# A decay vector fetched as one row and spread by three matmuls, in an attention and MLP kernel

## The chip, the core and the metric

The kernel runs on one core of one Trainium2 chip. The metric is the device time of one execution in microseconds (us). The core has five engines that run side by side, each with its own instruction queue: TensorE (PE, matmuls; its weight loads are listed as PEld), VectorE (DVE), ScalarE (ACT), GpSimd (POOL) and SyncE (SP, which here only issues transfers). Transfers run on 16 DMA engines. "SPq" and "ACTq" are the queues on which SP and ACT issue transfers.

## The reference

Two stages. First, linear attention with decay: 4 batches, 8 heads, 768 positions, 64 columns a head. Each head h has a decay `lam[h]` between 0.97 and 0.99. In blocks of 64 positions,

```
Dmask = where(rel >= 0, lam ** rel, 0)                 # rel = i - j inside a block
intra = ((q_b @ k_b.T) * Dmask) @ v_b
inter = (q_b * lam ** (pos + 1)) @ kv_state
out_b = intra + inter
kv_state = lam ** 64 * kv_state + (k_b * lam ** (63 - pos)).T @ v_b
```

The result, 3072 tokens of 512 columns, then goes through a two-layer MLP: `h = x @ w_in` (512 to 2048), `g = 0` below -1, `h` above 1, `(h + 1)^2 / 4` between, and `out = g @ w_out` (2048 to 512). Everything is float32 outside; the kernel computes in bfloat16 with float32 sums.

## The kernel before

The decay is folded into q and k: q is multiplied by `lam ** pos` and k by `lam ** -pos`, with pos counted from the middle of the 768 positions; the mask inside a chunk is then only causal. The powers come from tables. `lam` is loaded to all 128 partitions (`lam_b`, lines 92 and 93, a broadcast read issued by ACT), ACT takes its logarithm (`ln_lam`, L104), and `tables` (lines 111 to 118) makes two pairs of tables: DVE multiplies the logarithm by positions (`arg`, L113), ACT takes the exponentials (`tk`, L115, for k, and `tq`, L117, for q). The pair with suffix "e" serves the first stage below, the pair with suffix "d" all later chunks.

The work goes in this order:

- Units 0 to 3 (functions with the prefix `e_`) cover the first 512 positions of batch 0, in two halves of positions and two halves of heads. Each unit loads q, k and v on SP's queue (`e_load`, L302, tiles x0f, x1f, x2f, 256 KB each), casts them to bfloat16 with the tables (`e_cast`, L313 and L315: k on DVE, q and mostly v on POOL), transposes q and k on PE (`e_t`, L329), copies them back (L336), then computes scores (L373), masks them on DVE (L381), updates the state (L349), and sums the output (L393, L408) into `xT` (L419).
- Chunks 4 to 23 (prefix `f_`) cover the rest in 128 positions each, with loads at L426.
- The MLP runs in six strips of 512 tokens: first layer `f_l1` (L606) with its activation on ACT (L614) and DVE (L622 to L630), second layer `f_l2` (L639), results on L664 and stores. The weights are loaded by POOL (`load_w`, L152 for w_in, L153 for w_out, nine slices); the first slice waits for the landing of unit 2's k.

The order is not left to a scheduler: every step is entered with `add(...)` with its engine, an assumed duration, what it needs and a due time. `run_plan` (lines 174 to 267) plays this forward and issues the instructions in the order that comes out. The constants that concern the change: `DMA0` (L160), the planned time in ns at which the loads' stream begins; `T0` (L678), the due time of the first MLP step, from which nearly all due times are counted; the dictionary passed to `run_plan` (L884), when each engine is first free; and `WARM` (L269). Before and between PE's first planned steps, `run_plan` issues matmuls on zeros (`warm`, L275, "warm-ups"), from `WARM[0]` on, 512 columns each where there is room and 128 otherwise, until 200 ns before the next planned step on PE.

PSUM is divided into pools; `pp_h` (two banks) holds the warm-ups' output and later the first layer's, `pp_o` (one bank) the transposes of k and some attention outputs.

Of the kernel before, what the change touches and what calls it, by code (L numbers as in the profile page):

```python
# [8 lines left out]
F32 = mybir.dt.float32  # L9
BF16 = mybir.dt.bfloat16  # L10
I32 = mybir.dt.int32
AX = mybir.AluOpType
AF = mybir.ActivationFunctionType
# [10 lines left out]
def kernel(  # L24
# [16 lines left out]
    nc = tc.nc  # L41
    B, H, S, D = q.shape
# [8 lines left out]
    MS = 512  # L51
# [7 lines left out]
    RW, NR = 2, 3  # L59
    XT, MG, NQT, NQK, NVS, NUB, RING = 6, 6, 4, 4, 5, 4, 3.5  # L60
    DBG = False
    OB = 8

    const = ctx.enter_context(tc.tile_pool(name="const", bufs=1))
# [10 lines left out]
    rp = ctx.enter_context(tc.tile_pool(name="rp", bufs=NR))  # L75
    op = ctx.enter_context(tc.tile_pool(name="op", bufs=OB))
    PS = bass.MemoryType.PSUM
    pp_h = ctx.enter_context(tc.tile_pool(name="pp_h", bufs=2, space=PS))
# [3 lines left out]
    pp_o = ctx.enter_context(tc.tile_pool(name="pp_o", bufs=1, space=PS))  # L82
# [6 lines left out]
    SYNC = mybir.DependencyInfo(mybir.DependencyClass.Sync, mybir.DependencyReason.DATA)  # L89

    nc.scalar.preload_act_table_set("natural_log_exp_and_others")
    lam_b = const.tile([128, H], F32)
    nc.scalar.dma_start(out=lam_b, in_=lam.partition_broadcast(128))


    NE = 4
# [3 lines left out]
    make_identity(nc, ident)  # L100
    zz = const.tile([128, MS], BF16)
    nc.vector.memset(zz, 0.0)
    ln_lam = const.tile([128, H], F32)
    nc.scalar.activation(out=ln_lam, in_=lam_b, func=AF.Ln)  # L104
    pos_e = const.tile([128, NE], F32)
    nc.vector.tensor_copy(pos_e, pos_ei.rearrange("p a b -> p (a b)"))
    one = const.tile([128, 1], F32)
    nc.vector.memset(one, 1.0)  # L108


    def tables(pos, n, name):
# [11 lines left out]
    for t, base in ((mask2, 0), (mask2b, 128)):  # L123
        nc.gpsimd.memset(t, 1.0)
        nc.gpsimd.affine_select(
            out=t, in_=t, compare_op=AX.is_ge, fill=0.0,
# [7 lines left out]
        out=causal, in_=causal, compare_op=AX.is_ge, fill=0.0,  # L134
# [22 lines left out]


    LAT, FILL, SWITCH, NEAR = 100, 170, 105, 4000
    LEAD_Q, TAIL_Q, DMA0 = {"SP": 1300, "POOL": 1900}, 800, 3850  # L160
    ops, OPS = [], {}

    class Op:
# [5 lines left out]
    def add(key, eng, ns, fn, needs=(), due=None, extra=0, dma=0, perf=False, mode=("full", "full"), ring=1, slack=0, late=0):  # L169
        OPS[key] = Op(key, eng, ns, fn, list(needs), due, extra, dma, perf, mode, ring, slack)  # L170
        OPS[key].late = late
        ops.append(OPS[key])

    def run_plan(free):
# [42 lines left out]
        while len(out_seq) < len(ops):  # L217
# [33 lines left out]
            for u in users[x.key]:  # L251
                left[u.key] -= 1
                if left[u.key] == 0:
                    ready[u.eng].append(u)
        at, n1 = WARM[0], 0
        for t, _, x in sorted(out_seq, key=lambda p: p[:2]):
            if x.eng == "PE" and n1 < 2:
                while at < t - (200 if at < WARM[1] else WARM[2]):
                    one_ns = 58 if at > WARM[1] else 110
                    n = 4 if at + 4 * one_ns < t - 200 else 1  # L260
                    warm(n)
                    at += n * one_ns
                at = t + x.ns
                n1 += x.key[0] == "l1"
            if DBG:
                print(f"{t / 1e3:9.3f} {min(x.due, 9e6) / 1e3:9.3f} {x.eng:5s} {x.ns:6.0f} {x.end / 1e3:9.3f} {x.key}")
            x.fn()

    WARM = (1400, 7500, 700)  # L269
    wbank = []  # L270

    def warm(n):
        if not wbank:
            wbank.append(pp_h.tile([128, MS], F32, name="ph", tag="ph"))
        nc.tensor.matmul(wbank[0][:, 0:128 * n], lhsT=zz[:, 0:128], rhs=zz[:, 0:128 * n], start=True, stop=True, skip_group_check=True)  # L275

    def mm(*cols):
        return sum(c / 2.4 + 3 for c in cols)

# [372 lines left out]
    def f_ylast(part):  # L652
        cs = slice(CUT, d_model) if part else slice(0, CUT)
        if part == 0:
            osb["last"] = op.tile([128, d_model], F32, name="osb", tag="osb")
        nc.scalar.copy(out=osb["last"][:, cs], in_=py_t["last", part][:, cs])

    def f_stlast(part):
        cs = slice(CUT, d_model) if part else slice(0, CUT)
        nc.sync.dma_start(out=out[n_tok - 128:n_tok, cs], in_=osb["last"][:, cs])  # L660

    def f_y(s, ms):
        osb[s, ms] = op.tile([128, d_model], F32, name="osb", tag="osb")
        nc.scalar.copy(out=osb[s, ms], in_=py_t[s, ms])  # L664

    def f_out(s, ms):
        m0 = s * MS + ms * 128
        if s == 0:

            for j in range(2):  # L670
                nc.gpsimd.dma_start(out=out[m0:m0 + 128, :].rearrange("(p j) n -> j p n", j=2)[j], in_=osb[s, ms][HD[j], :])
        elif s < NST - 1:
            nc.gpsimd.dma_start(out=out[m0:m0 + 128, :], in_=osb[s, ms])  # L673
        else:
            nc.sync.dma_start(out=out[m0:m0 + 128, :], in_=osb[s, ms])


    T0, STEP, LEAD = 17000, 1035, 3000  # L678
    PARTS = {0: 2, 1: 4, 2: 2, 3: 2, 4: 2, 5: 2}
    W0 = [(w, p) for w in range(4) for p in range(2)]  # L680
    ALONE, AHEAD, AHEAD2 = 16, 6, 11
# [154 lines left out]
    for n1, (_, s, i, p) in enumerate(l1_order):  # L836
        prev = bank[on_y[n1]]
        n = PARTS.get(s, 1)
# [18 lines left out]
    for n2, (_, s, ms, kg) in enumerate(l2_order):  # L857
        n = PARTS.get(s, 1)
# [5 lines left out]
        if y == NCH - 1:  # L864
            if kg == 0:
                for part, n in ((0, CUT), (1, d_model - CUT)):
# [3 lines left out]
                    add(("y", y + part), "ACT", 400 - 240 * part, lambda part=part: f_ylast(part),  # L870
                        [("last", part), ("y", y - 1 + part), ("st", y - OB)], extra=95)
                    add(("st", y + part), "SP", 550 if s else 1100, lambda part=part: f_stlast(part), [("y", y + part), ("st", y - 1 + part)], due=-1,
# [5 lines left out]
        if kg == 3:  # L878
            add(("y", y), "ACT", 490, lambda a=(s, ms): f_y(*a), [("l2", n2), ("y", y - 1), ("st", y - OB)], extra=95)
            add(("st", y), "POOL" if s < NST - 1 else "SP", 1600 if s == 0 else 800 if s < NST - 1 else 550, lambda a=(s, ms): f_out(*a),  # L880
                [("y", y), ("o", 9 + y)] if s == 0 else [("y", y), ("st", y - 1) if y > CPS else None],
                due=l_due[2, s, ms, kg] + OLATE if s < NST - 1 else -1, dma=650, ring=0.2, slack=OSLACK if s < NST - 1 else 0)

    run_plan({"PE": 5000, "ACT": 5000, "DVE": 5000, "POOL": 5000, "SP": 800})  # L884


# [28 lines left out]
```

## Time and profile before

| what | value |
|---|---|
| time, median of 3 runs | 209.01 us (208.78 to 209.41) |
| time of the profiled execution | 210.35 us |
| its span, first to last instruction | 208.6 us |
| PE busy | 201.6 us, 97% of the span |
| DVE, ACT, POOL busy | 140.0, 120.4, 72.8 us |
| granted PE clock, mean over the span | 0.99 |
| DMA moved | 34.49 MB, mean 165 GB/s |

How to read what follows. The page divides the span into 40 slices of 5.2 us; each digit is a busy share in tenths, and the row PEclk is the granted share of PE's full clock. The chain of waits goes back from the last instruction, at each step to what released it. A timeline line gives the start, the duration, the engine, the line of the kernel, the operation with its output and inputs, and in brackets how long the engine had been idle and what ended that. A windows line gives the window, its length, the busy time of PE, PEld, DVE, ACT and POOL with the count of instructions, the granted clock, the DMA engines' busy share and GB/s. The clock's column covers what the trace recorded; before the first record, at 6.59 us, it shows 1.00 for want of one, while the warm-ups there take 0.427 us for 512 columns.

### The profile page before, as it was taken

Reading aid. Unit: us, or ns where it says so; the run is one execution under the profiler, and the core shown is the slowest. Engines: PE = TensorE matmul, PEld = TensorE weight load, DVE = VectorE, ACT = ScalarE, POOL = GpSimd, SP = SyncE. Lnnn points to the kernel's source line nnn. Section 1 sums busy time; section 2 is a strip of 40 time slices with the busy share of each in tenths; the row PEclk is TensorE's granted clock in tenths of the full one; section 3 lists DMA queues with packets and bytes.
Section 4 is the critical chain, followed back from the end, with each engine's and each line's share of the span. In section 5 each row is a group of like instructions: output and inputs, shape, how many; then the busy total and the mean of one; then the engine's idle time right before and its main releaser. Section 6 shows DMA issues by size and latency. Waiting matters only on the chain.

```text
span 208.6 us, 6389 instructions
## 1 busy us (share of the span) xinstructions
PE 201.6 (97%) x2754; PEld 137.1 (66%) x2754; DVE 140.0 (67%) x245; ACT 120.4 (58%) x225; POOL 72.8 (35%) x95
## 2 busy tenths in 40 slices
PE   7779999999999999999999999999999999999994
PEld 2457887446866876666766767667667666666643
DVE  0575697453898786998877989976866656354510
ACT  2564675225865767585675786575675565464421
POOL 5598200145255173763554354335511011010000
PEclk9996999999999999999999999999999999999999
DMA  4999999999999999999999999999822002011112
GB/s 106 296 246 177 201 202 199 234 214 179 173 232 211 196 235 222 212 246 228 173 199 280 170 257 219 205 177 213 147 50 104 3 5 98 0 50 53 50 50 101
DMA packets 95051, 34.49 MB, mean 165 GB/s; under 512 B 82352, under 2 KB 93360, under 8 KB 95024
## 3 DMA queue, kind: packets, MB, share of 16 engines
q1 hardware_dynamic: 88464, 24.65, 65.4%
q0 software_dynamic: 6416, 9.44, 21.2%
q8 instruction: 21, 0.34, 0.7%
q14 instruction: 6, 0.05, 0.1%
q10 hardware_dynamic: 144, 0.00, 0.0%
HBM read 27.27 MB, written 6.29 MB: 161 GB/s over the span
## 4 chain that ended last, share of the span: by engine, by line
PE 90%; SPq 4%; DMA 3%; ACT 1%; issue 1%; DVE 0%; ACTq 0%
PE ph L606 40%; PE py L639 39%; SPq L302 4%; DMA x1f<-in_k_dram 3%; PE py L649 2%; PE ps L500 1%; PE py L606 1%; PE ps L492 1%; PE pu L527 1%; PE po L527 1%; PE po L511 1%; PE py L408 1%; DVE ks L315 0%; PE pu L511 0%; PE py L393 0%
## 5 line engine op out<-in xcount | busy, mean ns | idle before, releaser
L606 PE MATMUL ph<-xT,w_in_sb 128*128 128x256 bf16 (+1 forms) x872 | 94.8, 258 | 0.0
L639 PE MATMUL py<-w_out_sb,gT 128*128 128x512 bf16 x368 | 91.1, 379 | 0.0
L614 ACT ACTIVATE r<-ph,one 128x512 bf16<-128x512 f32 x93 | 63.9, 687 | 46.5 <-PE ph L606 40.9
L606 PEld LDWEIGHTS <-w_in_sb 128*128 128x128 bf16 x896 | 76.7, 98 | 19.9 <-issue 0.2
L639 PEld LDWEIGHTS <-gT 128*128 128x128 bf16 x368 | 34.9, 98 | 28.4
L622 DVE TENSOR_SCALAR t<-r 128x1024 bf16<-128x1024 bf16 x48 | 24.9, 518 | 32.3 <-ACT r L614 32.1
L630 DVE TENSOR_TENSOR gT<-w,t 128x1024 bf16<-128x1024 bf16 x48 | 39.8, 830 | 1.4
L625 DVE TENSOR_TENSOR w<-r,t 128x1024 bf16<-128x1024 bf16 x48 | 36.9, 769 | 1.6
L453 POOL TENSOR_TENSOR kq<-x1f,tkd 128x512 bf16<-128x512 f32 x18 | 20.5, 1139 | 23.8 <-DMA x1f<-in_k_dram 21.7
L673 POOL DMA_DIRECT2D out_dram<-osb x16 | 9.1, 571 | 50.1 <-ACT osb L664 48.4
L453 POOL TENSOR_TENSOR kq<-x0f,tqd 128x512 bf16<-128x512 f32 x18 | 20.6, 1144 | 15.6 <-DMA x0f<-in_q_dram 15.4
L664 ACT COPY osb<-py 128x512 f32<-128x512 f32 x23 | 13.5, 587 | 12.1 <-PE py L639 11.4
L565 DVE TENSOR_TENSOR sd<-ps,diag 128x256 bf16<-128x256 f32 x36 | 13.5, 415 | 3.0 <-PE ps L500 3.0
L443 ACT CAST vs<-x2f 128x512 bf16<-128x512 f32 x20 | 12.3, 616 | 2.2 <-DMA x2f<-in_v_dram 2.2
L539 DVE TENSOR_TENSOR st<-st,ps 128x256 f32<-128x256 f32 x30 | 12.4, 414 | 0.5
L544 ACT CAST us<-st 128x512 bf16<-128x512 f32 (+1 forms) x18 | 10.5, 581 | 2.0 <-DVE st L539 1.8
L548 ACT CAST xT<-po 128x256 bf16<-128x256 f32 x18 | 6.8, 377 | 4.7 <-PE pu L511 4.1
L450 POOL TENSOR_TENSOR kq<-x0f,tqd 128x512 bf16<-128x512 f32 x2 | 2.1, 1040 | 20.1 <-DMA x0f<-in_q_dram 20.1
L548 ACT CAST xT<-pu 128x256 bf16<-128x256 f32 x18 | 6.7, 374 | 2.3 <-PE po L511 2.3
L527 PEld LDWEIGHTS <-vs 64*64 64x64 bf16 x288 | 3.7, 107 | 6.5 <-issue 5.9
L275 PE MATMUL ph<-zz 128*128 128x512 bf16 (+1 forms) x18 | 6.3, 510 | 1.3 <-DVE one L108 1.3
L381 DVE TENSOR_TENSOR sc<-ps,mask 128x512 bf16<-128x512 f32 x8 | 5.2, 681 | 2.4 <-PE ps L373 2.4
(89 smaller groups left out, 135.3 us busy)
## 6 DMA issues: line engine op xcount, KB each, us to landing
x0f<-in_q_dram SPq DMA_DIRECT2D x24, 256.0 KB, 5.6
x1f<-in_k_dram SPq DMA_DIRECT2D x24, 256.0 KB, 5.2
x2f<-in_v_dram SPq DMA_DIRECT2D x24, 256.0 KB, 5.5
out_dram<-osb POOLq DMA_DIRECT2D x16, 256.0 KB, 4.0
w_out_sb<-in_moe_w_out_dram POOLq DMA_DIRECT2D x4, 512.0 KB, 13.6
w_in_sb<-in_moe_w_in_dram POOLq DMA_DIRECT2D x3, 512.0 KB, 7.0
out_dram<-osb POOLq DMA_DIRECT2D x8, 128.0 KB, 4.4
out_dram<-osb SPq DMA_DIRECT2D x3, 256.0 KB, 2.0
```

Of the source, the lines that this page charges most:

```text
L443: (nc.scalar.copy if eng is nc.scalar else eng.tensor_copy)(t, qkv_ld[c, x])
L453: eng.tensor_tensor(t.rearrange("p (i g) d -> p g i d", g=2), qkv_ld[c, x].rearrange(h4, g=2), tb.rearrange(h4, g=2), op=AX.mult)
L539: nc.vector.tensor_tensor(st[c][:, a], st[c][:, 0] if a else st[c - 1][:, 1], kv[c][a], op=AX.add)
L548: nc.scalar.copy(out=get_xT(s)[:, :, off:off + 64], in_=po_of(c, a))
L565: nc.vector.tensor_tensor(sc_sb[c][:, par], pst[c, par], _bc(diag, 1, HP), op=AX.mult)
L606: nc.tensor.matmul(ph[:, j * m:(j + 1) * m], lhsT=w_in_sb[:, ko, (ni + j) * 128:(ni + j + 1) * 128], rhs=xT[s][:, ko, part * m:(part + 1) ...
L614: nc.scalar.activation(out=r_t[grp][:, i, :], in_=ph_t[s, ni, part], func=AF.Relu, bias=one[:, 0:1])
L622: nc.vector.tensor_scalar(t_t[grp], r, 0.5, 1.0, op0=AX.mult, op1=AX.min)
L625: nc.vector.tensor_tensor(w_t[grp], r, t_t[grp], op=AX.subtract)
L630: nc.vector.tensor_tensor(gT[s][:, f - RW * n:f, part * m:(part + 1) * m], w_t[grp].rearrange("p a (b m) -> p (a b) m", m=m), t_t[grp].rea ...
L639: nc.tensor.matmul(py_t[s, ms], lhsT=gT[s][:, ko, ms * 128:(ms + 1) * 128], rhs=w_out_sb[:, ko, :], start=(ko == 0), stop=(ko == FO - 1))
L664: nc.scalar.copy(out=osb[s, ms], in_=py_t[s, ms])
```

## The change

`lam` is fetched as one row of 8 numbers to one partition. DVE splits it into three bfloat16 parts (a rounded copy, the rounded rest, and the rounded rest of that: three copies and two subtractions). Three matmuls with a row of 128 ones as weights sum the parts in PSUM, which gives `lam` in all 128 partitions; ACT takes the logarithm from there. Five warm-ups are issued ahead of these matmuls, outside the plan, and the plan's own begin later. The tile in PSUM is the first one of the pool `pp_o`. Besides, the planner's constants for the start of the loads, the first due time, the warm-ups' limit and the engines' start are lowered.

```diff
+    WARM_LAM = 5
...
-    lam_b = const.tile([128, H], F32)
-    nc.scalar.dma_start(out=lam_b, in_=lam.partition_broadcast(128))
+    lam_1 = const.tile([1, H], F32)
+    nc.scalar.dma_start(out=lam_1, in_=lam.rearrange("(o h) -> o h", o=1))
...
-    ln_lam = const.tile([128, H], F32)
-    nc.scalar.activation(out=ln_lam, in_=lam_b, func=AF.Ln)
     pos_e = const.tile([128, NE], F32)
     nc.vector.tensor_copy(pos_e, pos_ei.rearrange("p a b -> p (a b)"))
     one = const.tile([128, 1], F32)
     nc.vector.memset(one, 1.0)
+    ones = const.tile([1, 128], BF16)
+    nc.vector.memset(ones, 1.0)
...
+    for _ in range(WARM_LAM):
+        warm(4)
+    lam_p = [const.tile([1, H], BF16, name=f"lam{i}") for i in range(3)]
+    lam_r = [const.tile([1, H], F32, name=f"lamr{i}") for i in range(2)]
+    lam_b = pp_o.tile([128, MS], F32, name="po", tag="po")[:, 0:H]
+    rest = lam_1
+    for i in range(3):
+        nc.vector.tensor_copy(lam_p[i], rest)
+        if i < 2:
+            nc.vector.tensor_tensor(lam_r[i], rest, lam_p[i], op=AX.subtract)
+            rest = lam_r[i]
+        nc.tensor.matmul(lam_b, lhsT=ones, rhs=lam_p[i], start=(i == 0), stop=(i == 2))
+    ln_lam = const.tile([128, H], F32)
+    nc.scalar.activation(out=ln_lam, in_=lam_b, func=AF.Ln)
...
-    LEAD_Q, TAIL_Q, DMA0 = {"SP": 1300, "POOL": 1900}, 800, 3850
+    LEAD_Q, TAIL_Q, DMA0 = {"SP": 1300, "POOL": 1900}, 800, 2850
...
-    WARM = (1400, 7500, 700)
...
+    WARM = (1400 + 440 * WARM_LAM, 6500, 700)
...
-    T0, STEP, LEAD = 17000, 1035, 3000
+    T0, STEP, LEAD = 16000, 1035, 3000
...
-    run_plan({"PE": 5000, "ACT": 5000, "DVE": 5000, "POOL": 5000, "SP": 800})
+    run_plan({"PE": 4200, "ACT": 4200, "DVE": 4200, "POOL": 4200, "SP": 800})
```

The function `warm` moves up unchanged, since it is now called before the plan.

More of the change, by code (lines that the diff above doesn't have):

```diff
@@ L108, with warm @@
     nc.vector.memset(one, 1.0)
+    ones = const.tile([1, 128], BF16)
+    nc.vector.memset(ones, 1.0)
+    wbank = []
+    def warm(n):
+        if not wbank:
+            wbank.append(pp_h.tile([128, MS], F32, name="ph", tag="ph"))
+        nc.tensor.matmul(wbank[0][:, 0:128 * n], lhsT=zz[:, 0:128], rhs=zz[:, 0:128 * n], start=True, stop=True, skip_group_check=True)
+    for _ in range(WARM_LAM):
[12 more added lines that the diff above has]
+    nc.scalar.activation(out=ln_lam, in_=lam_b, func=AF.Ln)
     def tables(pos, n, name):
@@ L267, in run_plan @@
             x.fn()
-    WARM = (1400, 7500, 700)
[L270 to L275, printed above, removed]
+    WARM = (1400 + 440 * WARM_LAM, 6500, 700)
     def mm(*cols):
```

## The prediction

> **What bounds the kernel now.** I read the page first, then the chain of waits, the timeline of the first 35 us, busy time in half-microsecond windows, and the trace's records of packets and landings. The page: TensorE (PE) is the bound, and from slice 4 on it never rests.
>
> ```profile
> PE   7779999999999999999999999999999999999994
> PEclk9996999999999999999999999999999999999999
> q10 hardware_dynamic: 144, 0.00, 0.0%
> ```
>
> Work that PE does while saturated can't shrink here; its start can move. PE fills at 16.6 us (windows: 19.96 to 20.00 us busy in each 20 us from 40 to 180). The 6 in PEclk is a stretch at half clock, 16.83 to 20.25 by the trace's clock records. What holds the start is told by the chain (start, duration, what): the queue of SP, then a load of k, then VectorE (DVE) and PE.
>
> ```profile
> 2.44 0.51 SPq L302
> 2.98 1.86 SPq L302
> 4.89 0.69 SPq L302
> ...
> 9.33 5.27 DMA x1f<-in_k_dram
> 14.62 1.01 DVE ks L315
> 15.67 0.40 PE po L329 x4
> ```
>
> SP issues a load each 0.55 us until its fifth sticks for 1.86 us; afterwards one each 0.7 to 0.9 us, as the transfers go. The landings in the trace are evenly spaced: 5.66, 6.58, 7.46, 8.39, 9.26 and so on to 14.60 for k of unit 3, 0.89 us apart. So the path is: when the stream begins, plus eleven loads, plus the arithmetic of unit 3. POOL and DVE wait for loads in every unit (0.33 and 0.29 us before the q casts, 0.76 and 0.37 before the k casts): they keep up.
>
> The windows show a slow start (last column GB/s, before it the DMA engines' busy share):
>
> ```profile
> 2.00:2.50 0.50, 0.50 (x2) 0.15 (x1) 0.00 (x0) 0.09 (x1) 0.50 (x2) 1.00 0.08 12
> 2.50:3.00 0.50, 0.50 (x3) 0.21 (x2) 0.00 (x0) 0.00 (x0) 0.43 (x2) 1.00 0.40 92
> 3.00:3.50 0.50, 0.50 (x3) 0.22 (x2) 0.00 (x0) 0.00 (x0) 0.44 (x2) 1.00 0.72 134
> 3.50:4.00 0.50, 0.50 (x3) 0.17 (x2) 0.00 (x0) 0.00 (x0) 0.35 (x4) 1.00 0.68 177
> 4.00:4.50 0.50, 0.50 (x2) 0.15 (x1) 0.00 (x0) 0.00 (x0) 0.24 (x1) 1.00 0.80 238
> 4.50:5.00 0.50, 0.50 (x2) 0.15 (x1) 0.00 (x0) 0.06 (x1) 0.00 (x0) 1.00 1.09 320
> ```
>
> The packets of lam (queue q10, 128 of 32 bytes and 16 that count) run from 1.94 to 4.60 us, spread over all that time among the loads' packets; the rate climbs as they thin out and is full in the half microsecond in which the last one goes. Each takes about 7 ns in the records, yet they come only one per 20 ns over all 16 engines. I read it so: 128 reads of the same 32 bytes are served one after another, and the loads queued on the same engines stand behind them.
>
> **The change, part by part.**
>
> *The broadcast becomes one row.* 128 reads become one to eight. From 2.0 to 4.5 us the windows moved (12+92+134+177+238) x 0.5 = 326 KB; at the 321 GB/s of 4.5 to 6.0 that takes 1.02 us, not 2.5: **1.48 us sooner** at most. If the first half microsecond (6 KB) is the stream's own ramp, the rest takes 1.0 us in place of 2.0: **1.0 sooner**. I take 1.2, the middle. Below it lies nothing at all, if the climb is the loads' own (a rival). SP's issues are no new limit: 0.55 us each against 0.89 for a transfer.
>
> A page speaks against this size. The Trainium skill, "DMA: Bandwidth & Descriptors", section "Measured (HBM→SBUF, 128 partitions, SWDGE, issued from GpSimd)", gives a 4 KB transfer to 128 partitions 0.68 us, and lam is 4 KB; by it no more than 0.68 us could be won, and the median would be 208.3. Here lam's packets, from ACT's queue and not GpSimd's, occupy 2.66 us: the trace disagrees, and I stay with the windows.
>
> *lam's new way to the tables.* Issue at 0.83 as now, first packet 1.94. A single packet lands between 2.3 (0.33 us after it, as after lam's last packet) and 2.9 (0.97, as after the first load's last). Five DVE operations on 1x8 follow: the nearest rows are a memset 128x1 of 0.06 us and a multiply 128x48 of 0.21, so 0.3 to 1.05. The three matmuls stand behind five warm-ups (L275, one each 0.427 us, from 1.32): not before 3.45. With 0.3 us to their reader, Ln starts at 3.8 to 4.3, against:
>
> ```profile
> 4.94 0.21 ACT L104 ACTIVATE ln_lam<-lam_b 128x8 f32<-128x8 f32 x1 [2.86 <-DMA lam_b<-in_lam_dram]
> 5.84 1.04 POOL L315 TENSOR_TENSOR qs<-x0f,tqe 128x512 bf16<-128x512 f32 x1 [1.60 <-ACT tqe L117]
> ```
>
> From Ln to the first q cast is 0.90 us now; so that cast starts at 4.7 to 5.2, 0.6 to 1.1 sooner. Its load would land at 4.5, so this cast waits for the tables and gains less than the loads. It doesn't matter by unit 1: POOL needs 1.04 + 0.61 us for a unit of q and v, the stream 2.64. Cast of q to 6.2, v of unit 0 (landed 6.26) to 6.9, and unit 1's q lands at 7.2. Even tables no earlier than today would have POOL back on the stream by unit 2. Cost at the end: nothing. Behind the waiting matmuls on PE stand only warm-ups; behind the waiting copies on DVE only the tables' multiplies. ACT waits for lam at the same place today.
>
> *Warm-ups.* Now 11 of 512 columns and 4 of 128, 1.26 to 6.56 us. After: 5, then, from 3600 in the loop to 200 short of the first planned transpose (5780), 4 and 2. These need 4 x 0.427 + 2 x 0.107 = 1.9 us; the first transposes come 2.3 us after lam's matmuls (0.3 to Ln, 0.9 to the cast, 1.1 of cast). The tail hides in that wait: nothing.
>
> *The plan's constants.* DMA0, T0 and the warm-up's end all drop by 1000, the engines' start by 800 (no engine but SP and PE's warm-ups has anything to do by then). Due times and ready times move together, so each choice of the planner stays as it is; only SP's seventh to ninth issue would have been planned under 1000 sooner, and those loads queue for the transfer anyway. I count the order as unchanged: nothing, and no queue is passed.
>
> *What is late next.* The weights: the first slice's issue on POOL follows unit 2's q cast and the landing of unit 2's k (11.97), so it moves too; it lands at 17.75, the first w_in matmul starts at 18.02, tight today and as tight after. Later slices have 2 us and more. All of it comes from the one stream, so the shift carries to the saturated stretch whole.
>
> **Sum.** Profiled execution: span 208.6, own time 210.35 (1.75 around it), 1.34 above the median 209.01. 210.35 - 1.2 = 209.15 (span 207.4); against the median, **207.8**.
>
> **The clock.** The half-clock stretch costs 1.2 to 1.7 us today: eight w_in matmuls take 1.82 us at 18.09 and 0.87 later, sixteen of L408 0.87 and 0.42. 3.41 us at half speed lose 1.7 of work; without it the first w_in matmul could begin only 0.27 sooner (slice at 17.75), and the saturated run that begins at 21.0 would begin near 19.8, so 1.2. I expect one such stretch after, as now. The Trainium skill, "TensorE: Matmul & The Clock Gate", "What's actually happening", says that the clock is judged in free-running windows of 3.4 us: the length agrees (3.41), whether it falls alike each time no row shows. By that rule the shorter warm-up could also leave the first window too empty for full clock, which comes at 6.59 today.
>
> **Rivals.**
> 1. *No half-clock stretch.* PE's work would fall otherwise into the windows: -1.2 more, **206.6**. For: PE was busy 2.6 of 3.41 us before the drop and 2.3 to 2.6 in windows without one: a near thing. Against: the same gaps remain, only earlier. 12%.
> 2. *The climb is the loads' own ramp.* q10's busy share is 0.0%: under 1.7 us over 16 engines, 0.1 each. Then only the tables come sooner, POOL still waits for loads, **208.9**. Against: full rate comes just with lam's last packet, and the engines idle (0.40 to 0.80) while SP's queue is stuck. 13%.
> 3. *Slower: a second half-clock window in the dense stage.* Each loses up to 1.7 us there. Two cost 2.4 to 3.4 where one costs 1.2 to 1.7; with the shift the net is 0 to +1.0, **209.7** where both fall on saturated work. It decides if the low window comes one later than now and holds for two. For: fewer warm-ups, a near thing as above. Against: after one such window PE was busy 3.41 of 3.41 and full clock returned at once. 10%.
> 4. *lam doesn't come sooner*: if the row lands at 4.9, the new copies and matmuls add 1.0 to 1.3 us, the first cast starts at 6.9 and POOL is behind to unit 2; with waits on the way I give it half the gain, **208.4**. 5%.
>
> **Numbers.** Forecast 207.8, chance 60%; its own range 207.3 to 208.3 (shift 1.0 to 1.5, and the runs' spread of 0.3). About 0.3%, 0.63 us, is what a measurement of this kernel can tell from no change. Faster by more: the forecast nearly whole (0.59), rival 1 (0.12), a little of 4: 0.72. Within: rival 2 and most of 4, some of 3: 0.19. Slower: 0.09. The range takes in part of rival 1 and rivals 2 and 4: 206.6 to 209.1.
>
> **What would show it.** Right: the rate is about 320 GB/s by 3.0 us, SP's fifth issue is no longer stuck, the first load lands near 4.5 and k of unit 3 near 13.4, PE fills near 15.4, one half-clock stretch. Wrong: the same climb without lam's packets (rival 2); landings sooner but PE saturated no sooner (a wait on tables, weights or clock); a second 5 or 6 in PEclk.

## The result, and the profile after

The changed kernel takes **208.14 us** (median of 20 runs, 207.50 to 210.20) against 208.94 for the kernel before, measured beside it in 20 runs (208.78 to 210.64): a ratio of 0.9963, with a 95% interval from 0.9945 to 0.9981. It is 0.8 us faster, not 1.2 as forecast (209.01 to 207.8). A run more than 1.5% above the fastest of its kernel counts as slow; the ratios here leave such runs out, the medians do not.

The profiled execution of the changed kernel is its fastest, 207.50 us with a span of 205.8; that of the kernel before was one of its long ones, 210.35 with 208.6. The two traces therefore differ by 2.8 us where the medians differ by 0.8. Lines in the new kernel stand 15 further down (L302 is L317, L606 is L621).

The page of the changed kernel, the rows that were shown of the kernel before:

```profile
PE   7789999999999999999999999999999999999994
PEclk9999999999999999999999999999999999999999
q10 hardware_dynamic: 2, 0.00, 0.0%
```

lam's queue moved 2 packets, not 144, and no half-clock stretch shows near 17 us. The windows of the loads' start (last column GB/s):

```profile
2.00:2.50 0.50, 0.50 (x2) 0.15 (x1) 0.49 (x1) 0.09 (x1) 0.50 (x2) 1.00 0.41 116
2.50:3.00 0.50, 0.50 (x3) 0.15 (x1) 0.43 (x3) 0.00 (x0) 0.43 (x2) 1.00 1.06 317
3.00:3.50 0.50, 0.50 (x2) 0.00 (x0) 0.43 (x3) 0.00 (x0) 0.44 (x2) 1.00 1.06 316
...
4.00:4.50 0.50, 0.50 (x2) 0.15 (x1) 0.45 (x3) 0.16 (x2) 0.26 (x1) 1.00 0.98 292
4.50:5.00 0.50, 0.50 (x3) 0.19 (x2) 0.13 (x1) 0.50 (x4) 0.23 (x1) 1.00 0.89 220
```

Full rate is there at 2.5 us, two microseconds earlier than before. But between 4.0 and 5.0 us the rate falls back, and with it the DMA engines' busy share. The first load lands at 3.76 us (5.66 before, 1.90 sooner), k of unit 3 at 13.13 (14.60, 1.47 sooner). The chain of waits, start, duration and what:

```profile
2.40 0.51 SPq L317
2.95 0.51 SPq L317
3.50 0.78 SPq L317
...
7.75 5.38 DMA x1f<-in_k_dram
13.16 0.92 DVE ks L330
...
16.19 1.04 PE ph L621 x8
...
18.21 0.98 PE ph L621 x8
```

SP's fifth issue is no longer stuck, the path is the same, and the saturated run begins at 18.2 us (21.0 before). Of these 2.9 us, 1.5 are the loads, the rest is the half-clock stretch that this execution lacks: eight w_in matmuls take 1.04 us at 16.19, and took 1.82. The new way to the tables in the timeline:

```profile
2.01 0.56 DVE L124 CAST lam<-lam 1x8 bf16<-1x8 f32 x1 [0.65 <-DMA lam<-in_lam_dram]
3.81 0.18 ACT L130 ACTIVATE ln_lam<-po 128x8 f32<-128x8 f32 x1 [1.72 <-PE po L128]
4.77 1.04 POOL L330 TENSOR_TENSOR qs<-x0f,tqe 128x512 bf16<-128x512 f32 x1 [0.51 <-ACT tqe L139]
```

The row is there at 2.01 us, Ln starts at 3.81 and the first q cast at 4.77: 1.1 us sooner each.

### The profile page after: what moved, and what is told of

It reads as the page before. It is cut to its first block, busy times and chain, and to the rows that moved or that the text cites. A ratio compares the mean times of both kernels' runs of the same rounds, so it can differ in the third digit from the quotient of the medians.

```text
span 205.8 us, 6360 instructions
## 1 busy us (share of the span) xinstructions
PE 196.9 (96%) x2721; PEld 135.7 (66%) x2753; DVE 140.8 (68%) x251; ACT 120.4 (59%) x225; POOL 72.3 (35%) x95
## 4 chain that ended last, share of the span: by engine, by line
PE 91%; SPq 3%; DMA 3%; issue 2%; DVE 0%; ACT 0%
PE ph L621 41%; PE py L654 38%; SPq L317 3%; DMA x1f<-in_k_dram 3%; PE py L664 2%; PE ps L515 1%; PE py L621 1%; PE ps L507 1%; PE pu L542 1%; PE po L542 1%; PE po L526 1%; PE py L423 1%; PE pu L526 0%; DVE ks L330 0%; PE ps L571 0%
## 5 line engine op out<-in xcount | busy, mean ns | idle before, releaser
L621 PE MATMUL ph<-xT,w_in_sb 128*128 128x256 bf16 (+1 forms) x872 | 94.0, 257 | 0.0
L629 ACT ACTIVATE r<-ph,one 128x512 bf16<-128x512 f32 x93 | 63.8, 687 | 45.2 <-PE ph L621 38.7
L621 PEld LDWEIGHTS <-w_in_sb 128*128 128x128 bf16 x896 | 76.3, 98 | 19.6 <-issue 0.2
L654 PE MATMUL py<-w_out_sb,gT 128*128 128x512 bf16 x338 | 86.0, 379 | 2.3 <-issue 1.1
L637 DVE TENSOR_SCALAR t<-r 128x1024 bf16<-128x1024 bf16 x48 | 22.5, 468 | 32.8 <-ACT r L629 32.4
L645 DVE TENSOR_TENSOR gT<-w,t 128x1024 bf16<-128x1024 bf16 x48 | 39.0, 812 | 1.4
L640 DVE TENSOR_TENSOR w<-r,t 128x1024 bf16<-128x1024 bf16 x48 | 38.8, 808 | 1.6
L468 POOL TENSOR_TENSOR kq<-x0f,tqd 128x512 bf16<-128x512 f32 x18 | 19.7, 1093 | 23.8 <-DMA x0f<-in_q_dram 23.7
L465 POOL TENSOR_TENSOR kq<-x0f,tqd 128x512 bf16<-128x512 f32 x2 | 2.4, 1178 | 20.8 <-DMA x0f<-in_q_dram 20.8
L515 PE MATMUL ps<-vs,kq 64*64 64x64 bf16 x264 | 6.2, 196 | 0.0
## 6 DMA issues: line engine op xcount, KB each, us to landing
w_out_sb<-in_moe_w_out_dram POOLq DMA_DIRECT2D x4, 512.0 KB, 14.4
```

The costliest lines, as they stand in the source:

```text
L468: eng.tensor_tensor(t.rearrange("p (i g) d -> p g i d", g=2), qkv_ld[c, x].rearrange(h4, g=2), tb.rearrange(h4, g=2), op=AX.mult)
L621: nc.tensor.matmul(ph[:, j * m:(j + 1) * m], lhsT=w_in_sb[:, ko, (ni + j) * 128:(ni + j + 1) * 128], rhs=xT[s][:, ko, part * m:(part + 1) ...
L629: nc.scalar.activation(out=r_t[grp][:, i, :], in_=ph_t[s, ni, part], func=AF.Relu, bias=one[:, 0:1])
L637: nc.vector.tensor_scalar(t_t[grp], r, 0.5, 1.0, op0=AX.mult, op1=AX.min)
L640: nc.vector.tensor_tensor(w_t[grp], r, t_t[grp], op=AX.subtract)
L645: nc.vector.tensor_tensor(gT[s][:, f - RW * n:f, part * m:(part + 1) * m], w_t[grp].rearrange("p a (b m) -> p (a b) m", m=m), t_t[grp].rea ...
```

## The experiments

Two numbers are followed through all traces: when k of unit 3 lands (k3), and from there to the end of the span. A kernel's time is its span and some 1.7 us.

| kernel | k3, us | span | k3 to the end | this execution | median |
|---|---|---|---|---|---|
| before | 14.60 | 208.62 | 194.02 | 210.35 | 208.94 |
| changed | 13.13 | 205.77 | 192.64 | 207.50 | 208.14 |
| e1 row and matmuls alone | 13.69 | 206.37 | 192.68 | 208.08 | 208.32 |
| e2 constants alone | 14.42 | 207.13 | 192.71 | 208.83 | 208.89 |
| e3 broadcast added | 14.42 | 207.52 | 193.10 | 209.25 | 209.45 |
| e4 128 far rows added | 14.26 | 208.08 | 193.82 | 209.78 | 208.58 |
| e5 changed, again | 13.75 | 206.40 | 192.65 | 208.10 | 208.33 |
| e6 queue of four | 15.11 | 210.43 | 195.32 | 212.13 | 210.63 |
| e7 queue of three | 15.36 | 208.69 | 193.33 | 210.38 | 213.09 |
| e8 no warm-ups | 13.71 | 207.43 | 193.72 | 209.13 | 208.50 |
| e9 loads later | 15.87 | 208.50 | 192.63 | 210.20 | 210.70 |
| e10 v, k, q | 14.23 | 207.67 | 193.44 | 209.37 | one run |
| e11 more warm-ups | 13.55 | 206.70 | 193.15 | 208.43 | 208.63 |
| e12 queue of four, end free | 14.37 | 208.34 | 193.97 | 210.05 | 210.05 |

Five traces agree on 192.63 to 192.71 us from k3 to the end, over a range of 2.7 us in k3: in these the end follows the landing of that one load one to one. The other traces lose more behind k3; where, is said with most of them (e10: PE pauses for 0.43 us at 101.9 behind a transfer that lands late).

**e1, the row and the matmuls alone.** The four constants of the planner are set back:

```diff
-    LEAD_Q, TAIL_Q, DMA0 = {"SP": 1300, "POOL": 1900}, 800, 2850
+    LEAD_Q, TAIL_Q, DMA0 = {"SP": 1300, "POOL": 1900}, 800, 3850
-    WARM = (1400 + 440 * WARM_LAM, 6500, 700)
+    WARM = (1400 + 440 * WARM_LAM, 7500, 700)
-    T0, STEP, LEAD = 16000, 1035, 3000
+    T0, STEP, LEAD = 17000, 1035, 3000
-    run_plan({"PE": 4200, "ACT": 4200, "DVE": 4200, "POOL": 4200, "SP": 800})
+    run_plan({"PE": 5000, "ACT": 5000, "DVE": 5000, "POOL": 5000, "SP": 800})
```

> The row and the three matmuls alone, with the planner's constants of before. The order of the work is that of the changed kernel; only two more warm-ups of 512 columns and two of 128 stand ahead of the first transposes (1.0 us more). Theory 1 (the loads' earlier stream is the whole gain, and the part of it that the median lacks, 0.5 to 0.7 us, is clock lost to the thinner warm-up): first load lands near 3.8 us, k of unit 3 near 13.1, and the median is 207.5 to 207.8, below the changed kernel's 208.14. Theory 2 (the missing part is lost later, to transfers or waits that vary from run to run, not to warm-ups): same landings, median 208.0 to 208.4. Theory 3 (the planner's constants bring part of the gain): 208.5 or more.

208.32 us (9 runs, 208.08 to 208.84), ratio 0.9959 (0.994 to 0.9979). Its instructions are those of the changed kernel in the same order, with four more warm-ups. So the gain is there without the constants (theory 3 falls), and more warm-ups don't bring the rest (theory 1's second half falls). The first load landed at 3.91 us, but k3 at 13.69, not 13.1: the median is theory 2's, but what is missing is lost in the loads.

**e2, the constants alone.** The opposite: the kernel before, with DMA0, T0 and the engines' start of the changed one, and

```diff
-    WARM = (1400, 7500, 700)
+    WARM = (1400, 6500, 700)
```

> The planner's constants alone, with the broadcast of before. The order stays, two or three warm-ups fewer ahead of the first transposes. Theory 1: landings as before (5.7 and 14.6 us); the time is that of before, 208.9, or up to 0.5 worse, 209.4, for clock lost to fewer warm-ups. Theory 2: 208.9. Theory 3: 208.5 or less.

208.89 us against 208.91, ratio 1.0004 (0.9991 to 1.0018): nothing. Its trace has a half-clock stretch twice as long as before's, from 8.78 to 15.61 us, yet it needs 192.71 us from k3 to the end: so early, half clock costs nothing.

**e3 and e4, is it the same address?** Behind the row, a transfer of the old broadcast's size into a tile that nobody reads, from the one row or from 128 rows of q:

```diff
+    dummy = const.tile([128, H], F32)
+    nc.scalar.dma_start(out=dummy, in_=lam.partition_broadcast(128))     # e3
+    nc.scalar.dma_start(out=dummy, in_=q[3, 7, 0:128, 0:H])              # e4
```

> The changed kernel with an additional transfer behind the row of lam: the old broadcast of lam to 128 partitions, into a tile that nobody reads. Theory 1 (128 reads of the same 32 bytes are served one by one and hold up the loads on the same engines): first load lands at 5.0 to 5.7 us and k of unit 3 at 14.3 to 14.7, the packets of the additional transfer go over some 2.6 us, and the median is 208.8 to 209.3. Rival (the slow start was the loads' own ramp, or the order of the queues): landings within 0.3 us of the changed kernel's, 208.1.

> The changed kernel with an additional transfer of the same size and packets, 128 times 32 bytes, but from 128 different rows of q, into a tile that nobody reads. Theory 1 (the same address is the trouble): packets go within 0.5 us, landings within 0.3 us of the changed kernel's (3.8 and 13.1), median 208.1 to 208.4. Rival (any 128 small packets at the start are as bad): first load at 5.0 or later, k of unit 3 at 14.3 or later, median 208.8 to 209.3.

Windows of e3:

```profile
2.50:3.00 0.50, 0.50 (x3) 0.15 (x1) 0.43 (x3) 0.00 (x0) 0.43 (x2) 1.00 0.99 293
3.00:3.50 0.50, 0.50 (x2) 0.00 (x0) 0.43 (x3) 0.00 (x0) 0.44 (x2) 1.00 0.90 189
3.50:4.00 0.50, 0.50 (x5) 0.28 (x5) 0.06 (x1) 0.18 (x1) 0.35 (x4) 1.00 0.54 162
4.00:4.50 0.50, 0.50 (x2) 0.15 (x1) 0.45 (x3) 0.17 (x2) 0.26 (x1) 1.00 1.04 142
```

and of e4:

```profile
2.50:3.00 0.50, 0.50 (x3) 0.15 (x1) 0.43 (x3) 0.00 (x0) 0.43 (x2) 1.00 0.96 281
3.00:3.50 0.50, 0.50 (x2) 0.00 (x0) 0.23 (x2) 0.00 (x0) 0.44 (x2) 1.00 1.19 322
3.50:4.00 0.50, 0.50 (x5) 0.28 (x5) 0.00 (x0) 0.18 (x1) 0.35 (x4) 1.00 1.08 319
4.00:4.50 0.50, 0.50 (x3) 0.15 (x1) 0.46 (x3) 0.17 (x2) 0.25 (x1) 1.00 0.96 247
4.50:5.00 0.50, 0.50 (x4) 0.26 (x3) 0.26 (x2) 0.50 (x4) 0.24 (x1) 1.00 0.95 208
```

In e3 the additional packets go from 2.91 to 5.16 us, and the loads run at about half rate from 3.0 to 5.0. In e4 the same number of packets goes from 2.94 to 3.38, and the rate is full from 3.0 to 4.0. So reads of one row are the trouble, and reads of 128 rows, 256 bytes apart, are not. The first load was ahead of the packets and landed at 3.78 in e3 too, which the expectation had missed; the second landed at 6.35.

e3 takes 209.45 us (1.0024, 1.0015 to 1.0034), e4 208.58 (0.9984, 0.9964 to 1.0003), both 0.15 to 0.2 above their ranges. Part of both is not the loads'. From the last copy of the output to the end of the span, all other traces need 2.51 to 2.53 us, e3 and e4 2.95 and 2.94; the copy in e1 and in e3:

```profile
203.58 0.27 ACT L671 COPY osb<-py 128x128 f32<-128x128 f32 x1 [0.42 <-PE py L664]
204.31 0.27 ACT L673 COPY osb<-py 128x128 f32<-128x128 f32 x1 [0.41 <-PE py L666]
```

SP waits there for the kernel's transfers one by one, and with one transfer more the last store is no longer the last of them: seven further waits of 0.06 us follow it. Without these 0.43 us the medians are 209.0 and 208.15, those of the kernel before and of the changed one. Between e3 and e4, which end alike, the one row costs 0.87 us.

k3 would not show that. It is nearly as late in e4 as in e3, where the expectation for far rows had 13.1, because of the fall of the rate that starts at 4.0 us, which by now stands in each trace without the broadcast. And e4's PE pauses for 0.72 us at 81.4, behind ACT, which had waited 1.82 us for a load of v.

**e5, the changed kernel again.**

> The changed kernel once more, for a second trace. Its first trace comes from its fastest run (207.5, k of unit 3 at 13.13 us); the runs so far without the broadcast show a slump of the stream between 4.0 and 5.9 us, at 600 to 1000 KB, of 0.4 to 1.3 us. If that slump is what the median lacks, then a run near the median (208.1) shows k of unit 3 at 13.5 to 13.9, PE saturated 5.0 us after that landing, and no loss behind. If the loss lies behind the start, the landing is at 13.1 and the distance from it to the end is longer than the 192.6 us of the first trace.

208.33 us (12 runs, 207.95 to 210.42), ratio 0.9986 (0.9965 to 1.0007); over both sets the changed kernel's 32 runs have a median of 208.22. The interval of this second ratio reaches past 1; four of its twelve runs took 209.07 us or more. This trace, of 208.10 us, stands near the median. Its windows:

```profile
3.00:3.50 0.50, 0.50 (x2) 0.00 (x0) 0.43 (x3) 0.00 (x0) 0.44 (x2) 1.00 1.15 344
3.50:4.00 0.50, 0.50 (x5) 0.28 (x5) 0.06 (x1) 0.18 (x1) 0.35 (x4) 1.00 1.03 302
4.00:4.50 0.50, 0.50 (x2) 0.15 (x1) 0.45 (x3) 0.16 (x2) 0.26 (x1) 1.00 0.76 184
4.50:5.00 0.50, 0.50 (x3) 0.19 (x2) 0.38 (x2) 0.50 (x4) 0.23 (x1) 1.00 0.82 206
5.00:5.50 0.50, 0.50 (x4) 0.23 (x2) 0.45 (x1) 0.04 (x1) 0.50 (x1) 1.00 0.90 256
```

and its chain at k of unit 3:

```profile
8.41 5.33 DMA x1f<-in_k_dram
13.77 0.99 DVE ks L330
```

Here the slump is deeper and longer than in the first trace: the third load lands 1.93 us after the second, where 0.9 is the rule. k3 is at 13.75, and 192.65 us follow. What this run near the median lacks against the fastest one is this slump, and nothing behind it.

**e6, e7 and e12, a shorter queue.** A load waits for the landing of the fourth (e6) or third (e7) before it; e12 is e6 with the last three loads free (`4 <= i < 9`):

```diff
         qkv_ld["e", u, x] = t
+        i = 3 * u + x
+        if i >= 4:
+            j = i - 4
+            tc.add_manual_dep(ld_dma["e", u, x].ins, ld_dma["e", j // 3, j % 3].ins.name, SYNC)
```

> The changed kernel with each load of the units issued only when the fourth before it has landed; the order stays. In every trace the slump, or the slow stretch of the broadcast, begins when the queue of SP is full for the first time (its sixth issue, 3.5 to 4.3 us, sticks). Theory A (the first filling of the queue costs the slump): the queue fills less or not, no window between 3 and 6 us is under 280 GB/s, k of unit 3 lands at 12.7 to 13.1, median 207.4 to 207.7. Theory B (the slump belongs to the transfers themselves): same slump, median 208.0 to 208.4.

> The same with the third before it: the queue is surely never full, but it may run dry, since an issue takes 1.1 us to its first packet and a landing comes 0.5 to 1.0 us after the last one. Theory A: no slump at 600 to 1000 KB; the stream may still be slower on the whole, by 0 to 0.3 us a load, so k of unit 3 at 12.8 to 16. Theory B: slump and gaps both, k of unit 3 at 13.6 or later, median 208.2 or more.

> The changed kernel with the fifth to ninth load each issued when the fourth before it has landed, and the last three at once. With all loads held back so, the ninth landed at 11.25 us (12.00 in the second trace of the changed kernel), but the last three were issued so late that they shared the DMA engines with the weights, and k of unit 3 landed at 15.11. If the shorter queue helps the stream and only those last three spoiled it: k of unit 3 at 12.9 to 13.3, and 192.65 us from there to the end give a median of 207.3 to 207.7, better than both kernels. If the earlier ninth load was chance: k of unit 3 at 13.6 to 13.9, median 208.1 to 208.4; gaps in the queue would make it later still.

Medians 210.63, 213.09 and 210.05; ratios 1.0025 (0.9994 to 1.0056), 1.0163 (1.0122 to 1.0204) and 1.0003 (0.997 to 1.0035). e6 and e12 are near neither of their expected times. The third load still lands 1.47, 1.14 and 1.65 us after the second, and the rate still falls; e6:

```profile
4.00:4.50 0.50, 0.50 (x2) 0.15 (x1) 0.45 (x3) 0.16 (x2) 0.26 (x1) 1.00 1.02 260
4.50:5.00 0.50, 0.50 (x3) 0.19 (x2) 0.33 (x2) 0.50 (x4) 0.23 (x1) 1.00 1.04 281
```

So theory A, that the first filling of the queue makes the slump, fails as it was put: without a full queue the slump is there. It isn't out altogether. The lowest window between 4 and 6 us is 260 GB/s in e6 and 255 in e12, against 184 in e5, 220 in the first trace of the changed kernel and 224 in e1; the queue may set how deep it goes. Both also have a second slump at 7.5 to 8.0 (187 and 164), and in e7 the queue of three may simply run dry. The waits open gaps of their own, the late loads share the DMA engines with the weights (issued from 10.73 us on in e6), and k3 comes at 15.11, 15.36 and 14.37. Behind it PE pauses once in e7 (0.78 us at 18.1) and twice in e12 (0.68 at 22.0, 0.46 at 38.7, both for slices of the weights). No better version came of it.

**e8, no warm-ups.** `for _ in range(WARM_LAM): warm(4)` becomes one `warm(1)`, and the plan issues none.

> The changed kernel without its warm-ups (one of 128 columns stays). If the clock in the first 15 us doesn't matter (the loads set the pace there) and full clock is there by the saturated stretch: 208.0 to 208.4. If the warm-ups are what brings full clock in time: half clock reaches into the saturated stretch, one window of 3.4 us there costs 1.2 to 1.7, so 209.3 to 209.9.

208.50 us (0.9981, 0.9964 to 0.9998), against 208.33 for the changed kernel on the same chip. In its trace full clock comes only at 17.05 us:

```profile
16.50:17.00 0.50, 0.50 (x15) 0.41 (x8) 0.26 (x1) 0.00 (x0) 0.50 (x2) 1.00 1.19 177
17.00:17.50 0.50, 0.40 (x25) 0.35 (x28) 0.00 (x0) 0.27 (x1) 0.50 (x1) 1.00 1.26 193
```

(the clock's column shows 1.00 before its first record; the counts of matmuls, 15 and then 25, show the step). From k3 to the end it needs 193.72 us, 1.07 more: that is the price of full clock at 17.05 in this run, a little under the 1.2 to 1.7 of a stretch in the saturated work. The median lies between the two expectations, nearer to the first.

**e9, the loads later.** The first load waits for POOL's second mask:

```diff
+        if u == 0 and x == 0:
+            tc.add_manual_dep(ld_dma["e", u, x].ins, m_ins.ins.name, SYNC)
```

> The changed kernel with its first load held back until POOL's first mask is made (2.3 us), so that the stream starts 1.5 us later and nothing else changes. If the slump belongs to the place in the stream (600 to 1000 KB, third and fourth load): it comes at 5.5 to 7.5 us, k of unit 3 lands near 15.2, median 209.5 to 209.9. If it belongs to the time since the start (4.0 to 5.9 us): the loads' rate is 290 GB/s or more in every window from 6.0 us on, k of unit 3 near 14.3, median 208.7 to 209.1.

210.70 us (1.0077, 1.0051 to 1.0103); k3 at 15.87, both above what was expected. The expectation counted on the first mask; the second is ready later, and the first load landed at 6.13, 2.37 after that of the changed kernel. The slump has moved with the stream:

```profile
5.00:5.50 0.50, 0.50 (x4) 0.22 (x2) 0.00 (x0) 0.04 (x1) 0.00 (x0) 1.00 1.15 346
5.50:6.00 0.50, 0.30 (x3) 0.04 (x1) 0.00 (x0) 0.00 (x0) 0.00 (x0) 1.00 1.19 344
6.00:6.50 0.50, 0.00 (x0) 0.00 (x0) 0.00 (x0) 0.00 (x0) 0.23 (x1) 1.00 0.87 246
6.50:7.00 0.50, 0.00 (x0) 0.00 (x0) 0.00 (x0) 0.00 (x0) 0.50 (x1) 1.00 0.63 162
```

PE, DVE and ACT do nothing in these last two windows, so the slump is not their doing; and it comes after some 1.3 us at full rate, not at a fixed time. POOL does work in them, from its first q cast at 6.27 on; in e5 the slump is there at 4.0, ahead of that cast (4.77).

**e10, another order in unit 0**, `(2, 1, 0) if u == 0 else (0, 1, 2)`; the planner orders later work otherwise, so the time (209.37, one run) isn't read.

> The changed kernel with the loads of unit 0 in the order v, k, q, not q, k, v. The planner then orders some later work otherwise, so only the stream is read from it, not the time. If the slump comes from v's place in memory, the first load is slow (lands after 4.3 us) and the third one is not (0.95 us or less after the second). If it comes from the place in the stream or from the time, the third load lands 1.1 to 2.3 us after the second, as v did.

Landings of v, k, q: 3.82, 4.70 and 6.74. The third load is the slow one again, now q: it is not v's place in memory.

**e11, more warm-ups** in PE's pauses: `WARM = (..., 6500, 200)`. The trace has 37 of them, where that of e3, with the changed kernel's, has 14: 23 more, most of 128 columns, and not eight as expected.

> The changed kernel with eight more warm-ups, in PE's pauses between the steps of units 0 to 3. If half-clock windows behind the warm-up are what lengthens some runs (208.6 to 210.4 in 8 of the 32 runs of the changed kernel), there are fewer of these and the median falls to 207.9 to 208.1. If they are not, or the pauses were too short for it: 208.1 to 208.4, same spread.

208.63 us (0.9979, 0.9963 to 0.9994), 12 runs from 208.36 to 209.13: no better than e5's 208.33 on another chip. No run is over 209.13, but only five of the 32 runs of the changed kernel are, so twelve runs can't tell whether the long ones are gone. In its trace k3 to the end takes 193.15 us, 0.5 more: three warm-ups (0.66 us from 15.37 on) stand ahead of the sums of unit 2, which start at 16.12; by their distance from k3 in e5 (2.03 us) it would be 15.58.

## Why the prediction was right, and where it was off

The sign and the mechanism were right. lam's broadcast held the loads up (e3), by reading one row 128 times (e4); the planner's constants bring nothing (e2), and the order stayed as counted; the path from k of unit 3 through PE to the end carries the shift whole (192.6 us in five traces); Ln and the first cast came at 3.81 and 4.77, inside their ranges, and the cast's wait for the tables left no trace in k3. That the reads are served one after another is not shown: their starts are uneven, 68 of the 128 within 3.0 to 3.5 us in e3. And not every unit's casts waited for loads: k of unit 1 (9.62 us) and q of unit 3 (13.98) started without a wait for one.

**The step that was mis-sized is the shift of the loads, "I take 1.2, the middle".** The start gained more than both its ends: the first load landed 1.90 us sooner, not 1.16. Then the stream, which I took to run on at 0.89 us a load from there, met the slump at its second to fourth load. In the trace near the median k3 is 0.85 us sooner (13.75 for 14.60; 0.67 against e2's 14.42), below my lower end of 1.0, and that is about the measured 0.8. The fastest run, with the mildest slump, has 1.47, close to the upper end of 1.48. So the time fell into the range partly by luck: the start was put 0.7 us too low, a loss of about 1 us behind it was not seen, and the two errors have opposite signs. The slump could not be seen in the trace of before: there the rate is 290 GB/s or more from 4.5 to 8.0 us, when over 1 MB has moved.

**The clock.** The stretch of before's profile cost 194.02 - 192.65 = 1.37 us, within the 1.2 to 1.7 predicted. But it isn't typical, as I had it: most runs of the kernel before take 208.8 to 209.1, which is the 208.8 to 209.0 that 14.4 to 14.6 us of loads and 192.65 give without any loss. I had forecast "one such stretch after, as now"; the first trace after has none. Where they lie counts: in e2, e5 and e9 they end by 16 us and cost nothing. Since I took the same loss off both sides, the sum against the median didn't suffer. The Trainium skill, "TensorE: Matmul & The Clock Gate", "What's actually happening", has the windows run freely: full clock was first granted at 6.59, 6.09, 4.47, 5.37, 4.56 and 5.43 us in the traces of before, after, e1, e2, e4 and e5, so the traces agree. That the shorter warm-up could leave full clock late came true now and then: at 14.22 us in e3 and 16.75 in e7, both with the changed kernel's warm-ups; that the shorter warm-up is the reason was not tested, since the kernel before was traced once. In the median it weighs little: with no warm-ups at all it is 0.17 us above e5's.

**The price of 4 KB.** The Trainium skill, "DMA: Bandwidth & Descriptors", section "Measured (HBM→SBUF, 128 partitions, SWDGE, issued from GpSimd)", gives 0.68 us for 4 KB to 128 partitions. The estimate from it was a median of 208.3. The measured one is nearer to that than to 207.8, but not for that reason: from one row the 128 packets take 2.25 us (e3), and from 128 rows 0.44 us (e4), somewhat less than the Trainium skill's figure.

**The rivals.** The own ramp (2) is out: full rate is there half a microsecond after the first packet. No half-clock stretch (1) was so in the profiled run, and it gives 207.5, not 206.6: the 206.6 took 1.2 us off a median whose typical run has no such stretch. lam late (4) is out: the row lands at 2.01, even sooner than the 2.3 to 2.9 that I gave it. A second stretch (3): of the 32 runs eight took 209.0 to 210.4 at mean clocks from 0.974 to 1.0, so something lengthens single runs by 1 to 2 us, but no trace of the changed kernel caught one, and its cause stays open. The trace of e6 shows what the rival meant: half clock from 15.62 to 22.45 us, two windows over the start of the saturated work, and 195.32 us from k3 to the end, 2.7 more than the rule, inside the 2.4 to 3.4 that I gave it.

**What stays open** is the slump. It follows the stream (e9), is not tied to one tensor (e10) nor to work on PE, DVE or ACT (e9), and comes without a full queue too, if shallower (e6, e12). It comes with single packets of 0.1 to 0.7 us where 0.03 is usual: six between 4 and 5 us in e5, none from 7 to 13. Its cause wasn't found.

## What to carry to other kernels

A small transfer ahead of a stream is priced by what it does to the engines that the stream shares, not by its own busy time: 4 KB with a busy share of 0.0% held 2 us of loads at half rate. Where a chain of loads sets the start of a saturated stretch, follow one landing on it through all traces: its distance to the end separates what the loads lost from what the rest lost. And look at which run a profile comes from before it is compared: these two were 2.8 us apart for 0.8 in the medians.

## What the runs showed of the hardware

128 reads of the same 32 bytes took 2.25 to 2.67 us in e3, e2 and before, a mean of one per 18 to 21 ns over all 16 DMA engines, and loads of 512-byte pieces beside them ran at 142 to 189 GB/s (e3, 3.0 to 5.0 us), where they ran at 317 without (changed kernel, 2.5 to 3.5); 128 reads of 32 bytes from rows 256 bytes apart were through in 0.44 us (e4). A stream of 256 KB loads that starts at 315 to 346 GB/s falls to between 160 and 260 GB/s for 0.5 to 1.8 us after the first 0.5 to 0.7 MB, in every trace without the broadcast. Copies of eight numbers on one partition from float32 to bfloat16 took DVE 0.26 to 0.56 us each, more than a copy of 128x4 (0.12); the five operations took 1.55 us, not 0.3 to 1.05, and ended at 3.56 us, level with the warm-ups ahead of the matmuls.
